# A new order for an attention-and-gMLP block: modulation products between identity products, Silu written as tanh, the last tile in unequal pieces

## The chip, the cores and the metric

One Trainium2 chip, one of its cores. The metric is the device time of one execution in microseconds (us); the time before is the median of three runs. The engines are named as in the profile: PE (TensorE, with PEld for its weight loads), DVE (VectorE), ACT (ScalarE), POOL (GpSimd), SP (SyncE, which here only issues DMAs).

## What is computed

A block with adaptive layer norm: S = 2048 rows, D = 448 columns, 16 heads of 28, a causal window of 256 keys, and a gated MLP of half-width 896 with a full S x S spatial product.

```
mod = silu(c) @ w_mod                      # 1 x 6*448: sa, ca, ga, sb, cb, gb
h = layernorm(x) * (1 + ca) + sa
q, k, v = split(h @ wqkv)                  # 16 heads of 28
p = softmax(mask(q k^T / sqrt(28)))        # key j of query i: 0 <= i - j < 256
x = x + ga * ((p @ v) @ wo)
h = layernorm(x) * (1 + cb) + sb
z = gelu(h @ w_in)                         # 2048 x 1792
z1, z2 = z[:, :896], layernorm(z[:, 896:])
g = w_sp @ z2 + b_sp
x = x + gb * ((z1 * g) @ w_out)
```

## The kernel before

The rows are cut into 16 tiles of 128, four tiles to a tile block. Every step (a product, a copy out of PSUM, a DMA) is recorded as an operation with the engines that may run it. A string, `ORDER` (lines 19 to 74), then lists all operations in sequence, each as a word of number, engine and buffer slots: "623.p.0" is operation 623 on PE with its first choice of bank. Each engine runs its own words in exactly that order, and waits by semaphores for what an operation needs. So the string alone decides on which engine a step runs and what stands in front of it.

The head loads x, the packed QKV weights and w_mod. Products of the identity with itself (L559) run on PE while nothing else is ready. The row c is turned into a column by four small products (L524), ACT applies Silu (L528, L529), and 32 products with the chunks of w_mod (L538) make the modulation column modT (L550, L551). The layer norm of a tile is statistics on DVE (L603, L606), a power on POOL (L611), a shift (L615) that only ACT's form of the norm needs, and the norm itself on DVE (L623), ACT (L625) or POOL (L628). QKV weights are copied into a padded layout WQK (L594, L595).

Tile block 0 goes in halves of two tiles: PE transposes xn (L679), the modulation is applied while hT is written out of PSUM (ACT L686, DVE L688), and QK products of 256 columns (L726) follow with the four chunks of D in the sequence 0, 1, 2, 3; their results go to qT and KT (L753, L754). Block 1 is transposed by PE too (L701, evicted at L715). Blocks 2 and 3 are transposed by DMA from SP's queue (L481, hT<-xn) and then modulated in place (L669 on ACT, L671 on DVE or POOL); their QKV products are L764, with copies out at L774 (ACT) and L775 (DVE). For block 3, K is copied in finer pieces (L793, L794). V is made at L801 and copied at L805 (ACT) and L806 (DVE).

Attention is S products (L876), exps on ACT (L909, L940), masks on DVE (L919, L955, L958), products with V (L984), a division (L997, L999), a DMA transpose of o_sb, the output product (L1007) and the residual (L1012). The second norm and its modulation (L1030 on ACT, L1032 on DVE or POOL) follow the same pattern. Then z2 and its gelu (L1063, L1074, L1086), z1 (L1109, L1117), the spatial products (L1133) against w_sp, which comes through 32 DMA transposes (wspA, wspB, also L481 on SP), the output products (L1152), the last sums (L1163, DVE) and the stores (L1168, SP). The last tile's output is made in three column pieces, 0 to 224, 224 to 336 and 336 to 448.

SP runs its DMA issues in order as well: a transpose of w_sp listed early is issued early.

Of the kernel before, what the change touches and what calls it, by code (L numbers as in the profile page):

```python
# [19 lines left out]
2.a 30.v 40.g 41.g 42.g 0.s 31.v 32.v 33.v 43.g 44.g 3.a 4.s 38.g 34.v 5.s 35.v 36.v 37.v 45.g 6.s 59.p.0 60.p.0 52.p.0 54.a 53.a 7.s 51.a 61.p.1 46.g  # L20
146.v 8.s 62.p.1 63.p.0 147.v 1.s 140.v 64.p.0 148.g 9.s 141.v 149.g 65.p.0 142.v 10.s 66.p.0 143.g 150.v 151.a.0 67.p.0 68.p.0 69.p.0 70.p.0 11.s
39.g 144.v 56.p.0 145.v.1 134.g 14.s 57.p 58.p 12.s 167.p.1 132.a 114.v 164.p.2 113.v 133.v 135.g 73.p.3 168.v 16.s 74.p.0 165.v 75.p.0 169.a 152.v
13.s 176.p.0.3 166.a 177.p.4.5 15.s 153.v 158.v 154.g 178.p 179.p 137.a 155.g 17.s 180.p 159.v 181.p 160.v 136.v 185.p 161.g 156.v 183.p 182.p 189.a
190.p.1.2 187.v 191.p.6.7 138.g 157.a.0 162.v 192.p 193.p 163.v.1 139.g 170.p.3 173.p.5 171.v 194.p 234.v 172.v 230.v 228.v 235.v 55.v 231.v 232.v
229.v 233.v 195.p 184.p 198.p 196.p 197.p 174.a 175.a 199.p 186.a 204.p.3 200.a 208.a 203.a 206.p.0 205.p.5 207.p.3 220.p.1 209.v 188.v 211.v 202.a
201.a 210.a 376.p.0.0 377.a.0 378.a 222.p.0 226.p.6 368.p.0.1 221.v 47.g 48.g 236.g 49.g 50.g 237.g 238.v 240.v.0 239.v.1 241.g.2 223.v 242.v.3 227.v
212.p.0 216.v 246.p.1 243.p.4 247.v 244.v 248.v 369.a.0 370.a 372.p.0.2 373.a 374.a 213.p.0 275.v 217.v 245.v 371.v 273.v 277.v 375.v 274.v 115.p.1
380.p.0.1 381.a.1 116.a 382.a 29.s 840.s 20.s 841.s 18.s 846.s 214.p.0 249.p.3 251.p.4 218.a 250.a 384.p.0.3 215.p.7 253.p.0 255.p.3 385.a 252.a 386.a
388.v 279.v 278.v 379.v 280.v 276.v 219.v 397.p.0.1 263.p.4 271.p.1 281.g 282.g 383.v 256.v 283.v 254.v 326.v 324.v 264.v 272.v 398.a.0 399.a
389.p.0.2 224.p.0 257.p.2 285.g.0 284.g.1 286.g.2 287.g.3 390.a.2 391.a 393.p.0.0 394.a 259.p.1 260.a 395.a 225.v 387.v 258.v 400.v 392.v 261.p.0  # L30
401.p.0.1 262.v 552.p.0 535.p.3 536.p 537.p 538.p 569.p.2 570.p 553.p 554.p 539.v 396.v 402.a.3 403.a 405.p.0.4 571.p 555.p 269.p.2 572.p 540.v.0
409.v 556.v 406.a 270.a 407.a 418.p.0.3 419.a.0 404.v 557.v.1 267.p.2 26.s 118.s 21.s 842.s 117.s 19.s 119.s 289.s 288.s 120.s 291.s 290.s 121.s 124.s
123.s 558.s 586.p.0 265.p.0 408.v 268.v 322.v 266.v 410.p.0.1 587.p 588.p 589.p 295.a 293.g 294.g 292.v 300.p.0 573.v 323.v 574.v.2 590.v 320.v 301.v
411.a.0 420.a 414.p.0.0 412.a 296.p.1 302.p.0 415.a 416.a 129.g 130.g 128.g 131.g 325.v 591.v.1 297.v 327.v 321.v 303.v 421.v 413.v 328.g 329.g 417.v
422.p.0.1 423.a.1 575.s 125.s 541.s 845.s 592.s 298.p.1 306.p.0 426.p.0.0 299.a 424.a 427.a 304.p.1 603.p.0 604.p 605.p 606.p 431.p.0.1 307.a 428.a
542.p.0 310.p.4 432.a.2 433.a 430.v 425.v 330.v 607.v 305.v 608.v.0 543.v 311.v 544.v 331.g.0 332.g.1 333.g.2 334.g.3 439.p.0.2 440.a.0 441.a 620.p.3
308.p.0 621.p 435.p.0.0 436.a 437.a 429.v 545.v 309.v 434.v 622.p 593.p.0 623.p 443.p.0.1 444.a.3 445.a 312.p.3 314.p.4 442.v 624.v 594.v 625.v.1
595.v 438.v 315.v 843.s 336.s 338.s 337.s 609.s 335.s 626.s 447.p.0.3 448.a 313.a 449.a 637.p.4 638.p 559.p.2 639.p 460.p.0.0 461.a.1 462.a 451.v
560.v 446.v 610.p.3 654.p.1 640.p 596.v 450.v 611.v 641.v 341.g 597.g 612.v 642.v.2 561.v 452.p.0.3 655.p 656.p 657.p 576.p.3 339.g 658.v 577.v 562.v
659.v.1 546.g 340.g 342.g 598.g 599.g 453.a.0 454.a 456.p.0.0 318.p.0 627.p.1 457.a 458.a 464.p.0.1 465.a.1 455.v 613.v 563.g 547.g 548.g 628.v 564.g  # L40
565.g 463.v 600.g.0 349.p.3 343.p.1 468.p.0.0 350.a 469.a 466.a 470.a 566.g.1 319.v 578.v 344.v 459.v 671.p.4 672.p 347.p.3 348.v 472.v 481.p.0.3
345.p.2 316.p.4 673.p 674.p 482.a.0 346.a 483.a 473.p.0.1 474.a.2 475.a 351.p.3 467.v 317.v 471.v 688.p.3 689.p 23.s 839.s 25.s 27.s 122.s 643.s 24.s
629.v 675.v 352.v 676.v.0 601.g 614.g 549.g.2 567.g 550.g 660.s 602.s 477.p.0.0 690.p 691.p 355.p.0 478.a 479.a 485.p.0.1 486.a.3 487.a 644.p.3
353.p.4 476.v 579.v 484.v 580.g 581.g 356.v 480.v 645.v 489.p.0.4 490.a 491.a 705.p.0 706.p 707.p 708.p 582.g 583.g.0 615.g 584.g 692.v 630.v 354.v
693.v.1 493.v 494.p.0.0 495.a.0 496.a 363.p.1 661.p.0 502.p.0.1 492.v 709.v 631.g 632.g 616.g 488.v 710.v.2 662.v 633.g 497.v 28.s 551.s 126.s 127.g
844.s 677.s 364.v 722.p.0 723.p 678.p.4 679.v 503.a.0 504.a 498.p.0.4 724.p 725.p 359.p.1 499.a 500.a 506.p.0.0 507.a.1 505.v 726.v 727.v.0 634.g.2
360.v 501.v 663.v 514.v 635.g 585.s 694.s 568.s 22.s 728.s 711.s 357.p.2 361.p.0 358.a 510.p.0.2 511.a 739.p.3 740.p 741.p 742.p 508.a 523.p.0.1
695.p.4 646.v 743.v 744.v.1 729.p.1 362.v 696.v 664.v 647.v 648.v 730.v 524.a.0 512.a 515.p.0.4 365.p.4 712.p.1 516.a.2 815.g 617.g.0 816.g 814.g
649.g 650.g 513.v 509.v 618.v 680.v 713.v 366.a 519.p.0.2 517.a 520.a 525.a 756.p.2 757.p 758.p 759.p 527.p.0.3 521.a 528.a.3 531.a 529.a 532.a 745.s
636.s 619.s 746.p.0 651.g.1 652.g 518.v 817.g 863.p.2 864.p.0 865.p 866.p 681.v 760.v 761.v.0 526.v 530.v 665.g 666.g 667.g 682.g 683.g 534.v 522.v  # L50
668.v.0 533.v 669.g 790.p.2 791.p 773.p.3 792.p 793.p 774.p 775.p 776.p 731.v 747.v 794.v 762.s 367.s 653.s 875.a 867.a 763.p.0 670.s 684.g 685.g.2
686.g 795.v.0 697.v 732.v 698.v 733.v 777.v 699.g 700.g 714.v 813.g 778.v.1 764.v 701.v 715.v 734.g 735.g 702.v.1 748.v 703.v 736.v.0 881.p.1 882.p.0
883.p 884.p 1003.p.2 1004.p.3 1005.p 1006.p 819.a 821.a 820.a 885.a 892.a 737.g 818.g 687.s 796.s 779.s 1008.a 1009.a 1007.a 898.p.1 899.p.0 900.p
901.p 1010.a 910.a 902.a 780.p.0 797.p.1 916.p.0 917.p.1 918.p 919.p 704.s 869.v 765.v 766.v 767.v 876.v 886.v 716.g 717.g 718.g 719.v.2 738.s 720.v
810.g 768.g 887.v 769.v 749.v 750.v 893.v 894.a.0 770.v.1 751.g 752.g 771.v 888.v 753.g.0 781.v 889.v 782.v 721.s 783.v 825.v 822.g 824.a 830.s 772.s
# [211 lines left out]
def bass_adaLN_cond__sliding_block__mixer_gmlp__prompt_kernel(  # L267
# [15 lines left out]
    NT = S // 128  # L283
# [361 lines left out]
    for tb in range(NB4):  # L645
# [84 lines left out]
        for hf in range(2 if tb == 0 else 0):  # L730
            for qk in range(2):
# [4 lines left out]
                if hf == 0:  # L736
# [6 lines left out]
                    for g in four:  # L743
                        last[g] = pe(MMH, [part(g, DC - 1, hq[g], hf)], [evh[hf], t_wqk[qk], done_], vv + 0.03 + 0.001 * g)
# [492 lines left out]
```

## Time and profile before

| what | before |
|---|---|
| median of 3 runs | 272.44 us (271.46 to 273.02) |
| the profiled execution's own time | 273.21 us |
| its span | 271.5 us |
| busy share of the span: PE, DVE, ACT, POOL | 96%, 59%, 49%, 46% |
| granted clock of TensorE | 1.00 |
| first QK product of block 0 | 8.62 us |
| DMA moved | 25.46 MB |

Time and span differ by 1.7 us, which lie outside of the profiled stretch. The busy shares are means over very different stages: the stretches that the prediction shows count for more. "PE busy" includes the identity products at the start, which compute nothing.

### The profile page before, as it was taken

The page shows a single profiled execution, that of the slowest core. Times are in us where ns is not written, and L with a number is a line of the kernel's source. Part 1 is how long each engine was busy: PE and PEld are TensorE (multiplying, and loading weights), DVE is VectorE, ACT ScalarE, POOL GpSimd, SP SyncE. Part 2 cuts the span into 40 slices and gives each one's busy share as a digit, 9 for nine tenths or more (in the row PEclk, how much of TensorE's full clock was granted, in tenths as well). Part 3 has the DMA queues.
Part 4 walks back from the last instruction along what each step waited for, and adds up shares of the span by engine and source line. Part 5 has one row for each costly group of instructions (what it writes and reads, how often), then busy time and mean ns, then how long its engine had stood idle before and what let it go on. Part 6 is the DMA issues. An engine that isn't in the chain of part 4 may idle for free.

```text
span 271.5 us, 6856 instructions
## 1 busy us (share of the span) xinstructions
PE 262.0 (96%) x2918; PEld 135.5 (50%) x2918; DVE 160.2 (59%) x357; ACT 132.2 (49%) x189; POOL 124.9 (46%) x184
## 2 busy tenths in 40 slices
PE   7898999999999999999999999999999999999995
PEld 3654455556476656444444444444444444444453
DVE  6898999999999999885746111123212102251233
ACT  3598999999999994799988300000000000000000
POOL 8530619325949668762499033445313100464130
PEclk9999999999999999999999999999999999999999
DMA  7998532857943567875999970000000000100203
GB/s 224 304 277 171 141 84 46 111 86 117 187 95 80 87 70 161 99 157 106 167 181 195 173 151 0 0 4 0 17 0 2 0 0 0 53 17 0 68 19 101
DMA packets 66777, 25.46 MB, mean 94 GB/s; under 512 B 57845, under 2 KB 66042, under 8 KB 66746
## 3 DMA queue, kind: packets, MB, share of 16 engines
q1 hardware_dynamic: 66472, 24.56, 47.1%
q8 instruction: 23, 0.38, 0.6%
q10 hardware_dynamic: 274, 0.46, 0.5%
q14 instruction: 8, 0.07, 0.1%
HBM read 9.53 MB, written 1.84 MB: 42 GB/s over the span
## 4 chain that ended last, share of the span: by engine, by line
PE 65%; DVE 21%; POOL 5%; ACT 5%; DMA 2%; issue 1%; DVEq 0%; POOLq 0%
PE ps L1133 36%; PE ps L1152 8%; PE ps L1109 7%; PE ps L1063 6%; DVE PA L919 4%; DVE PA L955 3%; DVE st_all L603 3%; PE ps L764 2%; ACT PA L909 2%; POOL rs_all L611 2%; DMA hT<-xn 2%; DVE Vaug L806 2%; PE ps L876 1%; PE ps L1007 1%; DVE o_sb L999 1%
## 5 line engine op out<-in xcount | busy, mean ns | idle before, releaser
L1140 POOL TENSOR_TENSOR z1T<-tmpg,z1T 128x512 bf16<-128x512 bf16 x28 | 31.8, 1154 | 76.2 <-DVE tmpg L1137 76.2
L909 ACT ACTIVATE PA<-ps 128x1536 bf16<-128x1536 f32 (+4 forms) x64 | 60.4, 974 | 2.7 <-PE ps L876 1.7
L1137 DVE TENSOR_TENSOR tmpg<-ps,bsp_bc 128x512 bf16<-128x512 f32 x28 | 19.0, 689 | 62.4 <-PE ps L1133 58.2
L1133 PE MATMUL ps<-wspB,z 128*128 128x512 bf16 x224 | 49.3, 379 | 0.0
L1133 PE MATMUL ps<-wspA,z 128*128 128x512 bf16 x224 | 49.2, 379 | 0.0
L1133 PEld LDWEIGHTS ps<-wspA,z 128*128 128x128 bf16 x224 | 21.8, 98 | 26.5 <-issue 0.4
L1133 PEld LDWEIGHTS ps<-wspB,z 128*128 128x128 bf16 x224 | 21.9, 98 | 26.3
L1163 DVE TENSOR_TENSOR fin<-ps,x_sb 128x448 bf16<-128x448 f32 (+2 forms) x18 | 10.0, 569 | 28.7 <-PE ps L1152 28.7
L611 POOL TENSOR_TENSOR rs_all<-ve_all,neghalf 128x1 f32<-128x1 f32 (+1 forms) x31 | 22.6, 732 | 5.2 <-DVE ve_all L608 3.3
L984 PEld LDWEIGHTS ps<-Vaug,PA 128*128 128x128 bf16 x720 | 20.4, 96 | 5.3 <-issue 1.3
L984 PE MATMUL ps<-Vaug,PA 128*128 128x32 bf16 x720 | 22.2, 176 | 0.4 <-DVE x_sb L1012 0.2
L1063 PE MATMUL ps<-w_in,hT 64*128 64x448 bf16 x224 | 22.3, 349 | 0.2 <-ACT z L1074 0.2
L1152 PE MATMUL ps<-w_out_g,z1T 128*128 128x448 bf16 (+2 forms) x126 | 22.2, 332 | 0.0
L1109 PE MATMUL ps<-hT,w_in 64*128 64x512 bf16 x196 | 21.8, 376 | 0.0
L919 DVE TENSOR_TENSOR PA<-PA,mask 128x1024 bf16<-128x1024 bf16 (+1 forms) x32 | 21.7, 683 | 0.0
L764 PE MATMUL ps<-hT,WQK 128*128 128x512 bf16 x80 | 19.6, 380 | 0.5 <-DVE hT L671 0.5
L603 DVE BATCH_NORM_STATS2 st_all<-x_sb 128x6 f32<-128x448 bf16 x32 | 19.3, 611 | 0.0
L876 PE MATMUL ps<-qT,KT 32*64 32x64 bf16 (+3 forms) x768 | 17.9, 223 | 0.9 <-ACT PA L909 0.3
L608 POOL TENSOR_SCALAR ve_all<-mv_all 128x1 f32<-128x1 f32 (+1 forms) x19 | 6.5, 344 | 25.2 <-DVE mv_all L606 21.0
L940 ACT ACTIVATE PA<-ps 128x1536 bf16<-128x1536 f32 (+1 forms) x16 | 16.4, 1027 | 1.7 <-PE ps L876 1.5
L955 DVE TENSOR_TENSOR PA<-PA,mask 128x2048 bf16<-128x2048 bf16 x14 | 17.0, 1215 | 0.0
L1152 PEld LDWEIGHTS ps<-w_out_g,z1T 128*128 128x128 bf16 x126 | 11.7, 98 | 10.1 <-POOL z1T L1140 0.2
(115 smaller groups left out, 334.7 us busy)
## 6 DMA issues: line engine op xcount, KB each, us to landing
w_in<-in_B_w_in_dram SPq DMA_DIRECT2D x8, 224.0 KB, 4.1
out_dram<-fin SPq DMA_DIRECT2D x15, 112.0 KB, 1.7
x_sb<-in_A_x_dram SPq DMA_DIRECT2D x3, 448.0 KB, 5.3
wmod<-in_w_mod_dram SPq DMA_DIRECT2D x1, 1344.0 KB, 9.7
w_out_g<-in_B_w_out_dram SPq DMA_DIRECT2D x1, 784.0 KB, 5.1
bsp_bc<-in_B_b_sp_dram SPq DMA_DIRECT2D x1, 512.0 KB, 4.3
x_sb<-in_A_x_dram SPq DMA_DIRECT2D x2, 224.0 KB, 3.4
wmod<-in_w_mod_dram SPq DMA_DIRECT2D x2, 224.0 KB, 5.3
```

The costliest lines, as they stand in the source:

```text
L603: st = [dve(0.62 if True else 0, lambda e, t=t, ci=ci, s=s: e.bn_stats(st_all[:, slot, t, ci, :], s()), deps(t), prio) for ci, s in enumer ...
L611: rs = pool(0.41 + 0.155 * len(tiles), lambda e: e.tensor_tensor(rs_all[:, slot, a:b], ve_all[:, slot, a:b], neghalf[:, 0:b - a], ALU.pow) ...
L764: m = pe(4 * MMS, [lambda e, h=h, g=g, kc=kc, tb=tb: e.matmul(ps[:, h.slot[0], :], lhsT=WQK[:, kc, 4 * g:4 * g + 4, :].rearrange("p a b -> ...
L909: return e.activation(cols(place(kb, hf) + 64 + 768 * a, [[384, 2 * (b - a)], [1, w]]), ps[:, h.slot[0]:h.slot[0] + b - a, 2 * n * w:(2 * ...
L919: main_mk[(kb, hf)] = dve(0.15 + 512 * tri / 1920.0, lambda e, hf=hf, tri=tri: e.tensor_tensor(cols(place(kb, hf) + 64, [[384, 8], [192, t ...
L955: return e.tensor_tensor(cols(a, [[d, 2], [384, 16], [1, 64]]), cols(src(), [[0, 2], [64, 16], [1, 64]]), mask_ap([[64 if m else 192, 2], ...
L984: fns.append(lambda e, hO=hO, hd=hd, bi=bi, kb=kb, nb=nb, j=j, c=(2 * t + k) * 384 + 128 * (j - kb), half=half: e.matmul(ps[:, hO.slot[0], ...
L1063: return lambda e, kc, p0, start, stop: e.matmul(ps[:, hs[t % 2].slot[hf], 0:D], lhsT=hT[p0:p0 + 64, kc, t * 128:(t + 1) * 128], rhs=w_in[ ...
L1109: return lambda e, kc, p0, start, stop: e.matmul(ps[:, hs[b // 2].slot[b % 2], :], lhsT=w_in[p0:p0 + 64, kc, ft * 128:(ft + 1) * 128], rhs ...
L1133: m = pe(16 * MMS, [lambda e, h=h, si=si, ft=ft, tb=tb: e.matmul(ps[:, h.slot[0], :], lhsT=z2[:, si, ft * 128:(ft + 1) * 128], rhs=(wspA i ...
L1140: u = pool(1.16, lambda e, ht=ht, ft=ft, tb=tb: e.tensor_tensor(z1T[tb][:, ft, :], tmpg[:, ht.slot[0], :], z1T[tb][:, ft, :], ALU.mult), [ ...
L1152: return [lambda e, ft=ft: e.matmul(ps[:, h.slot[0], c0:c1], lhsT=z1T[t // 4][:, ft, (t % 4) * 128:(t % 4 + 1) * 128], rhs=w_out_g[:, ft, ...
```

## The change

There are six edits, of which the new order holds the most.

1. `c_row` is padded to four full chunks and the constant `one` becomes 0.5, so that PSUM holds c/2. ACT takes its tanh (in the table set that the exps use), and one DVE instruction makes (tanh + 1) times c/2, which is silu(c). One load of a table set falls away.
2. The identity products are cut differently (`warm(9, ...)`, `warm(45, ...)`: 17 in all instead of 15), and the products with w_mod run partly between them, chunk by chunk.
3. In tile block 0 the odd tiles' norm runs only on DVE, and needs no shift. The copies out of the transposes are paired as chunks (2, 0) and (1, 3).
4. The QK products of block 0 take the chunks in the sequence 2, 1, 0, 3.
5. The last tile's pieces are 0 to 224, 224 to 384 and 384 to 448, and the middle piece's store is issued by ACT's queue.
6. `ORDER` is new throughout. A main mask may run on POOL by the new code; the new order doesn't use that.

```diff
-    t_p1 = [dve(0.1, lambda e: e.memset(one[:], 1.0), prio=-99.0), dve(0.1, lambda e: e.memset(sc_sb[:], 0.0), prio=-98.9)]
+    t_p1 = [dve(0.1, lambda e: e.memset(one[:], 0.5), prio=-99.0), dve(0.1, lambda e: e.memset(c_row[:, D:DP], 0.0), prio=-98.9)]
...
-    t_sc = [
-        act(0.25, lambda e: e.activation(sc_sb[:, 0:3], ps[:, hC.slot[0], 0:3], ACT.Silu), [t_cT, t_p1], -90.0, table="silu"),
-        act(0.25, lambda e: e.activation(sc_sb[0:64, 3:4], ps[0:64, hC.slot[0], 3:4], ACT.Silu), [t_cT, t_p1], -90.0, table="silu"),
-    ]
-    hC.until += t_sc
+    t_th = act(0.25, lambda e: e.activation(th[:], ps[:, hC.slot[0], 0:DC], ACT.Tanh), [t_cT], -90.0, table="exp")
+    t_sc = dve(0.2, lambda e: e.scalar_tensor_tensor(sc_sb[:], th[:], 1.0, ps[:, hC.slot[0], 0:DC], ALU.add, ALU.mult), [t_th], -90.0)
+    hC.until += [t_th, t_sc]
...
-    warm(14, [], 0.44, 1)
-    warm(40, [], 0.22, 1)
+    warm(9, [], 0.43, 1)
+    warm(45, [], 0.215, 1)
...
+        if not share and t % 2:
+            return add({"dve": (0.39, on_dve)}, deps, prio, [h])
...
-            for cp in range(2):
+            for cp, chs in enumerate(((2, 0), (1, 3))):
...
+        FIRST = (2, 1, 0, 3)
+
         def part(g, kc, h, hf):
             return lambda e: e.matmul(ps[:, h.slot[0], 0:256], lhsT=WQK[:, kc, 4 * g:4 * g + 4, :].rearrange("p a b -> p (a b)"),
-                                      rhs=hT[:, kc, hf * 256:(hf + 1) * 256], start=(kc == 0), stop=(kc == DC - 1))
+                                      rhs=hT[:, kc, hf * 256:(hf + 1) * 256], start=(kc == FIRST[0]), stop=(kc == FIRST[-1]))
...
-            for c0, c1 in ((0, D // 2), (D // 2, 3 * D // 4), (3 * D // 4, D)) if t == NT - 1 else ((0, D),):
+            for c0, c1 in ((0, D // 2), (D // 2, D - 64), (D - 64, D)) if t == NT - 1 else ((0, D),):
...
-                o = add({"sp": (0.4, lambda e, hf=hf, t=t, c0=c0, c1=c1: e.dma_start(out_d[:, t, c0:c1], fin[:, hf.slot[0], c0:c1]))},
+                o = add({"act" if c0 == D // 2 else "sp": (0.4, lambda e, hf=hf, t=t, c0=c0, c1=c1: e.dma_start(out_d[:, t, c0:c1], fin[:, hf.slot[0], c0:c1]))},
```

Of the order itself, three places. First PE's queue in the head (ident is the identity, L559 or L558 its products with itself; wmod the modulation weights; L679 or L680 the transposes of block 0; WQK the QK weights). Before:

```order
L559 MATMUL ps<-ident 128x512 x10
L542 MATMUL ps<-xn,ident 128x8
L538 MATMUL ps<-sc_sb,wmod 128x1 x32
L679 MATMUL ps<-ident,xn 128x128 x8
L559 MATMUL ps<-ident 128x512 x3
L726 MATMUL ps<-hT,WQK 128x256 x23
L679 MATMUL ps<-ident,xn 128x128 x8
L726 MATMUL ps<-hT,WQK 128x256 x25
```

and now:

```order
L558 MATMUL ps<-ident 128x512 x6
L541 MATMUL ps<-xn,ident 128x8
L537 MATMUL ps<-sc_sb,wmod 128x1 x8
L558 MATMUL ps<-ident 128x512 x3
L537 MATMUL ps<-sc_sb,wmod 128x1 x24
L680 MATMUL ps<-ident,xn 128x128 x8
L558 MATMUL ps<-ident 128x512 x2
L729 MATMUL ps<-hT,WQK 128x256 x12
L558 MATMUL ps<-ident 128x512
L729 MATMUL ps<-hT,WQK 128x256 x2
```

Eight products with w_mod moved ahead of three identity products, and some identity products moved in among the first QK products.

Second, SP's queue behind the head's first loads (wspA is half of w_sp, wo_g the output weights of the attention, mod_rows a copy of the gates in DRAM). Before:

```order
L409 DMA x_sb<-in_A_x_dram 128x4x448
L450 DMA wo_g<-in_A_wo_dram 64x448
L481 DMA_TRANSPOSE wspA<-in_B_w_sp_dram 128x1024
L405 DMA wo_g<-in_A_wo_dram 64x448
L481 DMA_TRANSPOSE wspA<-in_B_w_sp_dram 128x1024
L409 DMA x_sb<-in_A_x_dram 128x4x448
L481 DMA_TRANSPOSE wspA<-in_B_w_sp_dram 128x1024
L445 DMA w_in<-in_B_w_in_dram 128x896
```

and now:

```order
L410 DMA x_sb<-in_A_x_dram 128x4x448
L406 DMA wo_g<-in_A_wo_dram 64x448
L410 DMA x_sb<-in_A_x_dram 128x4x448
L405 DMA wo_g<-in_A_wo_dram 128x3x448
L576 DMA mod_rows<-gg_sb 1x448 x4
L451 DMA wo_g<-in_A_wo_dram 64x448
L576 DMA gg_sb<-mod_rows 128x448
L576 DMA modT<-mod_rows 128x3x1
L482 DMA_TRANSPOSE hT<-xn 128x4x128 x4
```

The transposes of w_sp moved behind the loads of x, the gates and the first transposes of hT.

Third, POOL's queue once block 2's norms begin (L628 or L629 the norm, L671 or L672 the modulation of hT, L587 or L586 the gate on the output weights). Before:

```order
L628 TENSOR_SCALAR xn<-x_sb,rs_all,ve_all 128x448
L608 TENSOR_SCALAR ve_all<-mv_all 128x4
L611 TENSOR_TENSOR rs_all<-ve_all,neghalf 128x4
L628 TENSOR_SCALAR xn<-x_sb,rs_all,ve_all 128x448 x4
L671 TENSOR_SCALAR hT<-hT,modT 128x512 x2
L587 TENSOR_TENSOR wo_g<-wo_g,gg_sb 128x448 x4
L608 TENSOR_SCALAR ve_all<-mv_all 128x4
L611 TENSOR_TENSOR rs_all<-ve_all,neghalf 128x4
L628 TENSOR_SCALAR xn<-x_sb,rs_all,ve_all 128x448 x4
```

and now:

```order
L607 TENSOR_SCALAR ve_all<-mv_all 128x4
L610 TENSOR_TENSOR rs_all<-ve_all,neghalf 128x4
L629 TENSOR_SCALAR xn<-x_sb,rs_all,ve_all 128x448 x2
L586 TENSOR_TENSOR wo_g<-wo_g,gg_sb 128x448 x4
L607 TENSOR_SCALAR ve_all<-mv_all 128x4
L610 TENSOR_TENSOR rs_all<-ve_all,neghalf 128x4
L629 TENSOR_SCALAR xn<-x_sb,rs_all,ve_all 128x448 x2
L672 TENSOR_SCALAR hT<-hT,modT 128x512 x2
```

The other two norms of each block and most of the modulation moved to DVE's queue. Over the attention, up to the last mask, DVE has 11 steps of the norm on tiles of x instead of 5 and 6 modulations of hT instead of 1, and gives copies out of PSUM to ACT: KT in 512 columns 4 instead of 6, KT in finer pieces 2 instead of 4, qT in 512 columns 6 instead of 7, V 10 instead of 12.

More of the change, by code (lines that the diff above doesn't have):

```diff
@@ L24 @@
[L24 to L31, printed above, removed]
@@ L518, in bass_adaLN_cond__sliding_block__mixer_gmlp__prompt_kernel @@
     t_mask.append(pool(0.2, lambda e: e.tensor_copy(mask01[:, 4, :], mask01[:, 0, :]), [t_mask[0]], -84.0))
-    t_pre = act(0.2, lambda e: e.activation(zero[:, 1:2], zero[:, 0:1], ACT.Silu), [t_p0], -98.8, table="silu")
+    t_pre = act(0.2, lambda e: e.activation(zero[:, 1:2], zero[:, 0:1], ACT.Tanh), [t_p0], -98.8, table="exp")
     hC = Hold(bM)
-    t_cT = pe(0.5, [lambda e, ch=ch, m=m: e.matmul(
-        ps[0:m, hC.slot[0], ch:ch + 1], lhsT=c_row[:, ch * 128:ch * 128 + m], rhs=one[:, 0:1], start=True, stop=True)
-        for ch, m in ((0, 128), (1, 128), (2, 128), (3, 64))], [t_c, t_p1[0]], -91.0, [hC])
-    t_sc = [
-        act(0.25, lambda e: e.activation(sc_sb[:, 0:3], ps[:, hC.slot[0], 0:3], ACT.Silu), [t_cT, t_p1], -90.0, table="silu"),
-        act(0.25, lambda e: e.activation(sc_sb[0:64, 3:4], ps[0:64, hC.slot[0], 3:4], ACT.Silu), [t_cT, t_p1], -90.0, table="silu"),
-    ]
-    hC.until += t_sc
+    t_cT = pe(0.5, [lambda e, ch=ch: e.matmul(
+        ps[:, hC.slot[0], ch:ch + 1], lhsT=c_row[:, ch * 128:ch * 128 + 128], rhs=one[:, 0:1], start=True, stop=True)
+        for ch in range(DC)], [t_c, t_p1], -91.0, [hC])
+    t_th = act(0.25, lambda e: e.activation(th[:], ps[:, hC.slot[0], 0:DC], ACT.Tanh), [t_cT], -90.0, table="exp")
+    t_sc = dve(0.2, lambda e: e.scalar_tensor_tensor(sc_sb[:], th[:], 1.0, ps[:, hC.slot[0], 0:DC], ALU.add, ALU.mult), [t_th], -90.0)
+    hC.until += [t_th, t_sc]
     t_screp = dve(0.5, lambda e: e.tensor_copy(sc_rep[:], sc_sb[:].unsqueeze(2).broadcast_to([128, DC, 32])), [t_sc, t_x[1]], -16.0)
@@ L652, in bass_adaLN_cond__sliding_block__mixer_gmlp__prompt_kernel @@
             tiles = [4 * tb + i for i in half]
-            r = stats(0, tiles, lambda t: [lambda: x_sb[:, t, :]], lambda t: [t_x[t // 4] if t >= 4 else t_x0[t // 2]], v_e)
+            r = stats(0, tiles, lambda t: [lambda: x_sb[:, t, :]], lambda t: [t_x[t // 4] if t >= 4 else t_x0[t // 2]], v_e, tb > 0 or tiles[0] % 2 == 0)
             for t in tiles:
```

126 lines of the change are left out of this document (68 added, 58 removed).

## The prediction

> **What bounds the kernel now.** I read the page's first part, then the busy time by stretches, then the chain that ended last, then the waits of the stretches in which TensorE is not full. The stretches (columns: stretch, length, busy time and count of PE, PEld, DVE, ACT, POOL, granted clock, DMA share, GB/s):
> ```profile
> 8.60:25.00 16.40, 13.63 (x197) 8.82 (x197) 14.04 (x39) 12.63 (x21) 5.50 (x12) 1.00 1.15 273
> 25.00:100.00 75.00, 73.25 (x1502) 42.86 (x1499) 74.30 (x144) 71.99 (x83) 42.32 (x58) 1.00 0.58 99
> 114.50:150.50 36.00, 36.00 (x345) 16.81 (x346) 24.19 (x75) 32.51 (x61) 22.85 (x44) 1.00 0.94 161
> 150.50:268.40 117.90, 117.90 (x576) 55.43 (x574) 27.64 (x44) 2.56 (x5) 35.74 (x32) 1.00 0.13 30
> 268.40:271.50 3.10, 0.18 (x4) 0.01 (x1) 0.62 (x3) 0.00 (x0) 0.00 (x0) 1.00 0.26 74
> ```
> From 114.5 to 268.4 TensorE has no gap, 153.9 us in two rows, and the granted clock is 1.00 throughout. The change leaves the work of that stretch as it is, so nothing can be won there. What can move is the head (16.40 − 13.63 = 2.8 us without TensorE work), the attention (25 to 100), where PE, DVE and ACT are all full to within 3.0 us, and the 3.1 us of the tail. POOL is the one engine with room in the attention: 42.32 of 75. The chain through the head and the tail (start, length, what):
> ```profile
> 7.32 0.41 PE ps L679 x4
> 9.36 1.28 PE ps L726 x10
> 11.09 0.35 DVE ve_all L615
> 11.46 0.90 DVE xn L623
> 12.40 0.41 PE ps L679 x4
> 21.38 1.09 issue
> 268.27 0.37 DVE fin L1163 x2
> ```
> The second half of the transposes of tile block 0 waits for one DVE norm of 0.90 us (L623, tile 3), and at 21.38 TensorE's queue stands 1.09 us for nothing that the profile shows. TensorE's own timeline gives the waits beside them:
> ```profile
> 12.40 0.62 PE L679 MATMUL ps<-ident,xn 128*128 128x128 bf16 x8 [0.80 <-DVE xn L623]
> 12.86 1.15 PE L726 MATMUL ps<-hT,WQK 128*128 128x256 bf16 x9
> 14.28 1.92 PE L726 MATMUL ps<-hT,WQK 128*128 128x256 bf16 x16 [0.27 <-ACT hT L686]
> 22.47 0.23 PE L701 MATMUL ps<-ident,xn 128*128 128x128 bf16 x1 [1.09 <-issue]
> ```
>
> **The change part by part.** All terms are against the profiled execution, 273.21 us, which lies 0.77 above the median of 272.44; the sum is then put onto the median.
>
> *Head, modulation products and Silu.* The products as such and the ACT work are the same size; Silu as tanh loads one table set fewer. That load was off the path:
> ```profile
> 16.43 1.28 ACT L940 ACT_TABLE_LOAD   x1
> 18.09 2.08 ACT L940 ACTIVATE PA<-ps 128x1536 bf16<-128x1536 f32 x2 [0.38 <-PE ps L876]
> 7.32 0.62 PE L679 MATMUL ps<-ident,xn 128*128 128x128 bf16 x8
> 7.78 0.81 PE L559 MATMUL ps<-ident 128*128 128x512 bf16 x3
> ```
> The first exp waited after the load for TensorE (0.38), so the 1.28 us are worth nothing at that place; they free ACT for evictions, which I count in the attention. The three identity products at 7.78 fill the time until hT is there; in the new order nine products of this kind stand ahead of the first transposes after the c products, and six more behind these transposes and among the first QK products. Each costs 0.27 by that row, and they stand where TensorE would wait for hT: 0, and up to +0.5 if two of them delay a ready product. Starting QK with chunk 2 moves which eviction is first, not how many: 0 (±0.2).
>
> *Head, norms.* Tile 3's norm waits for a shift step (L615) that only ACT's form of the norm needs; without it DVE saves part of the 0.35 row. But DVE now makes three of the first hT evictions instead of two ahead of the statistics of tiles 2 and 3, which puts those about 0.35 later, and ACT no longer takes a norm. POOL has one WQK copy less beside the norm of 0.90. Against this stands the row of that form over the whole run:
> ```profile
> L623 DVE TENSOR_SCALAR xn<-x_sb,mv_all,rs_all 128x448 bf16<-128x448 bf16 x12 | 6.3, 535 | 0.7 <-DMA hT<-xn 0.4 <-POOL ve_all L618 0.2
> L671 DVE TENSOR_SCALAR hT<-hT,modT 128x512 bf16<-128x512 bf16 x1 | 1.2, 1202 | 0.0
> L1032 DVE TENSOR_SCALAR hT<-hT,modT 128x512 bf16<-128x512 bf16 x5 | 1.8, 402 | 0.0
> ```
> A norm of the mean 0.535 instead of 0.90 gives −0.37. I take −0.3 for the second transposes, between 0 and −0.7. The wait ahead of 14.28 (the gap between the end of the row at 12.86 and it is 0.27) goes if the evictions pair as (2,0) and (1,3) with one of each pair on DVE: −0.3 (0 to −0.4).
>
> *The queue that stands at 21.38.* The transfers in that window (queue, packets, MB, share; the issue and its time to landing):
> ```profile
> q1 hardware_dynamic: 3712, 1.68, 122.7%
> q8 instruction: 1, 0.02, 0.8%
> wspA<-in_B_w_sp_dram SPq DMA_TRANSPOSE x3, 6.2
> ```
> Three transposes of the spatial weights are in the DMA engines from 16 to 24 us, and the one block of code of that window comes through the same engines. The new order issues none of them until the transposes of hT for tile block 2 are out, so I read the gap as code that came late, and take it as gone: −1.1 (0 to −1.1). The Trainium skill, Runtime: NRT & Kernel Launch, section Instruction fetch mechanics, says that a sequencer fetches its next page on a queue of its own while it executes, and that this is hidden by the pace of issue. By that sentence the gap would be something else and would stay, and the sum below would be 1.1 us less; the row at 21.38 speaks against full hiding, but does not name its cause. What the moved transposes cost: they now land during the attention (DMA share 0.58), and behind the last transposes of hT the new order leaves 19 of this kind where 23 stood, ahead of the spatial products that read them; I take 0, and up to +1 if the last ones come late.
>
> *Attention.* These are the steps that change engine (line, engine, form, count, total and mean ns):
> ```profile
> L774 ACT ACTIVATE qT<-ps 128x512 bf16<-128x512 f32 x5 | 3.1, 621 | 0.0
> L774 ACT ACTIVATE KT<-ps 128x512 bf16<-128x512 f32 x2 | 1.2, 610 | 0.0
> L805 ACT ACTIVATE Vaug<-ps 128x448 bf16<-128x448 f32 x4 | 2.2, 545 | 0.0
> L775 DVE CAST KT<-ps 128x512 bf16<-128x512 f32 x6 | 4.1, 676 | 0.1
> L806 DVE CAST Vaug<-ps 128x448 bf16<-128x448 f32 x12 | 7.2, 611 | 0.0
> L671 POOL TENSOR_SCALAR hT<-hT,modT 128x512 bf16<-128x512 bf16 x6 | 6.3, 1052 | 12.8 <-DMA hT<-xn 12.8
> L628 POOL TENSOR_SCALAR xn<-x_sb,rs_all,ve_all 128x448 bf16<-128x448 bf16 x18 | 13.9, 782 | 4.4 <-DVE ve_all L615 4.0
> ```
> DVE takes over 11 tensor_scalar steps up to the attention's last mask (xn from 5 to 11, hT from 1 to 6): 11 x 0.402 = 4.4 us at the free price, 11 x 0.535 = 5.9 at the norm's mean. It gives off four KT casts, of which two are of the finer form, and one of qT, 5 x 0.676 = 3.4, and two of Vaug, 2 x 0.611 = 1.2: net 0 to +1.3. ACT takes what DVE gave off, 5 x 0.61 + 2 x 0.545 = 4.1 by the means (records of one engine overlap at their ends, so 3.3 is the least), against 75 − 71.99 = 3.0 us of its idle time in the stretch. If all of the idle time could be used the end comes 0.3 to 1.1 later; if none, 3 to 4; and as the first exps come earlier (no table load ahead of them, other products first), some of it starts before 25. I take +0.9, between −1 and +3. POOL's relief, some 11 x 0.8 to 1.0 us, is worth nothing by itself.
>
> *Transition and tail.*
> ```profile
> ACT z L1086 <- PE ps L984: 3.4, 1, 3.4
> 267.91 1.94 SPq L1168 DMA_DIRECT2D out_dram<-fin  x4
> 267.82 0.75 PE L1152 MATMUL ps<-w_out_g,z1T 128*128 128x112 bf16 x12
> 268.27 0.75 DVE L1163 TENSOR_TENSOR fin<-ps,x_sb 128x112 bf16<-128x112 f32 x3 [0.39 <-PE ps L1152]
> ```
> ACT waits 3.4 us ahead of the first gelu; the new order has it modulate hT in that hole: −0.2 (0 to −0.4). At the end SP issues four stores back to back, 1.94/4 = 0.48 each, and the last of three pieces stands behind two others. With the middle piece on ACT's queue the last one issues one slot earlier, −0.48, and its DVE piece is 64 columns instead of 112; against that, the middle piece is larger (160 columns). I take −0.4 (−0.6 to +0.1).
>
> The sum: −0.3 − 0.3 − 1.1 + 0.9 − 0.2 − 0.4 = −1.4. From 273.21 that is 271.8, and put on the median, 272.44 − 1.4 = **271.0** us. Adding the helpful and the harmful ends by squares rather than singly gives about −3 to +1 for this case, 269.4 to 273.4.
>
> **The rivals.** *DVE's moved steps are blocked by POOL.* DVE's one L671 step ran beside two POOL products:
> ```profile
> 43.00 2.04 POOL L587 TENSOR_TENSOR wo_g<-wo_g,gg_sb 128x448 bf16<-128x448 bf16 x2
> 43.99 1.20 DVE L671 TENSOR_SCALAR hT<-hT,modT 128x512 bf16<-128x512 bf16 x1
> ```
> It took 1.202 us where the same shape at L1032 takes 0.402: a loss of 0.80 a step. The change puts 11 more such steps on DVE inside the stretch in which DVE has 0.7 us of room (74.30 of 75). If every second one loses, 5.5 x 0.80 = 4.4, less the 1.4: +3.0, **275.4**. It decides from 4 of 11 on (3.2 − 1.4 = +1.8, over 0.5%). For it: those rows. Against: the mean of 0.535 over twelve norms is a loss of 0.13 each, by which 11 lose 1.5, and POOL has less to do afterwards. The Trainium skill, SBUF — State Buffer, section Who interferes with whom, says that a tensor_scalar of the fast kind and GpSimd take one pair of ports as an exclusive lock, so that whoever issues second waits out the whole instruction; the 1.202 us agrees with it, being about the free time plus a POOL step, and it speaks against this change. Chance 0.30.
>
> *Only the tail moves.* The head's gain is taken back because DVE and ACT set the attention's end in any case; what stays is −0.4: **272.0**. For it: both engines are full from 25 to 100. Against: their work starts earlier with the head. Chance 0.12.
>
> *POOL's relief counts in full.* If POOL's serial work (xn, then hT) was what delayed the QKV products of blocks 2 and 3, the 3.0 us of idle time of ACT and the 1.75 us of PE in the stretch go, and the head's 2.8 too: about −4, **268.4**. For it: a POOL step is 0.782 and 1.052 where DVE needs 0.40. Against: DVE has little room to take it. Chance 0.18.
>
> **How the numbers follow.** A measurement of this kernel can tell about 0.5%, 1.36 us, from no change: 271.08 and 273.80 are the bounds. The forecast has 0.40; its centre lies at the lower bound, so 0.24 of that is faster, 0.14 within, 0.02 slower. Faster: 0.24 + 0.18 from the third rival = 0.42. Within: 0.14 + 0.12 from the tail rival + 0.02 from the mild end of the first = 0.28. Slower: 0.02 + 0.28 = 0.30. The likeliest case alone spans 269.4 to 273.4; the range of 8 in 10 reaches down to the third rival's centre and up just past the first's, 268.4 to 275.6.
>
> **What would show it.** Right: second L680 group near 12.0 and no issue gap of 1 us near 21; DVE's xn and hT tensor_scalar rows at 0.40 to 0.55; the gap-free stretch of TensorE beginning about a microsecond earlier; the last store issued by 0.7 us after TensorE's end. The first rival: those DVE rows at 0.8 to 1.2 and masks late, and the exps ending later than before. The tail rival: the exps end where they did. Wrong altogether: a gap in TensorE between 114 and 268, which no term here has, for instance from spatial weights that land late, or a head in which QK starts later than 8.6.

## The result: slower by 1.0%

| | before | after |
|---|---|---|
| median | 272.48 us (270.91 to 273.02, 6 runs) | 274.88 us (273.28 to 276.65, 6 runs) |
| ratio, 95% interval | | 1.0103 (1.0054 to 1.0151) |
| profiled execution, span | 273.21, 271.5 | 273.28, 271.4 |

The changed kernel is about 2.8 us slower, with an interval of 1.5 to 4.1. Its profiled execution happens to be the fastest of its six, and that of before was slower than each of its six: the two traces end at the same moment, and alone they would show no change. So a second trace was taken of the changed kernel (below, 276.06). Executions more than 1.5% slower than the fastest of the same kernel are left out of the ratios and their intervals, while the medians and ranges hold all executions.

The busy time by stretches in the first trace after (columns as in the prediction):

```profile
8.60:25.00 16.40, 15.96 (x273) 10.58 (x274) 15.54 (x46) 13.63 (x26) 5.45 (x12) 1.00 0.76 234
25.00:100.00 75.00, 69.60 (x1449) 41.83 (x1456) 73.03 (x149) 72.35 (x84) 33.29 (x46) 1.00 0.59 105
100.00:114.50 14.50, 14.50 (x218) 8.33 (x220) 13.59 (x34) 10.80 (x19) 9.03 (x15) 1.00 1.01 172
114.50:150.50 36.00, 35.57 (x340) 16.47 (x338) 24.94 (x72) 31.38 (x60) 24.59 (x50) 1.00 0.95 163
150.50:268.40 117.90, 117.27 (x557) 54.80 (x564) 27.71 (x43) 2.47 (x5) 33.66 (x30) 1.00 0.13 26
```

The head has become dense (15.96 of 16.40 where before had 13.63), though identity products are in it. What it won is gone by 100: TensorE has 69.60 of 75 where it had 73.25 (some missing records may be in that difference). DVE and ACT are nearly as full as before (73.03 against 74.30, 72.35 against 71.99), and POOL has 9 us less to do. From 114.5 on TensorE's rows are 1.1 us short of full, with 24 records fewer than before.

DVE's moved steps, grouped by form (count, total us, mean ns), in the same trace:

```profile
L622 DVE TENSOR_SCALAR xn<-x_sb,mv_all,rs_all 128x448 bf16<-128x448 bf16 x21 | 8.8, 432 | 1.9 <-POOL ve_all L617 1.0 <-POOL rs_all L610 0.6
L672 DVE TENSOR_SCALAR hT<-hT,modT 128x512 bf16<-128x512 bf16 x4 | 2.1, 543 | 0.0
L1036 DVE TENSOR_SCALAR hT<-hT,modT 128x512 bf16<-128x512 bf16 x8 | 2.8, 384 | 0.0
```

They are at 0.38 to 0.54, near the free price, not at 0.8 to 1.2: the broad form of the first rival did not happen here. DVE now waits 1.9 us ahead of norms, though (0.7 before), most of it for small steps on POOL.

The tail, in the timeline:

```profile
267.73 1.65 DVE L1167 TENSOR_TENSOR fin<-ps,x_sb 128x448 bf16<-128x448 f32 x4 [0.70 <-PE ps L1156]
269.24 0.37 ACTq L1172 DMA_DIRECT2D out_dram<-fin  x1
```

TensorE ends at 269.05 and the span at 271.44, 2.39 us later; before it was 268.58 and 271.46, 2.88. The tail gained 0.49.

### The profile page after: what moved, and what is told of

Its sections match the earlier page's. It is cut to its first block, busy times and chain, and to the rows that moved or that the text cites. A ratio compares the mean times of both kernels' runs of the same rounds, so it can differ in the third digit from the quotient of the medians.

```text
span 271.4 us, 6838 instructions
## 1 busy us (share of the span) xinstructions
PE 260.4 (96%) x2901; PEld 135.9 (50%) x2920; DVE 161.3 (59%) x365; ACT 134.5 (50%) x195; POOL 111.0 (41%) x167
## 4 chain that ended last, share of the span: by engine, by line
PE 70%; DVE 18%; ACT 6%; POOL 4%; issue 2%; POOLq 0%; DVEq 0%
PE ps L1137 35%; PE ps L1156 8%; PE ps L1067 8%; PE ps L1113 6%; ACT PA L912 4%; DVE PA L922 3%; PE ps L1011 3%; PE ps L988 2%; DVE st_all L602 2%; DVE PA L959 2%; POOL rs_all L610 2%; PE ps L558 2%; DVE xn L622 2%; DVE Vaug L809 1%; PE ps L879 1%
## 5 line engine op out<-in xcount | busy, mean ns | idle before, releaser
L1156 PE MATMUL ps<-w_out_g,z1T 128*128 128x448 bf16 (+3 forms) x126 | 22.0, 332 | 0.0
L988 PE MATMUL ps<-Vaug,PA 128*128 128x32 bf16 x720 | 21.6, 176 | 0.4 <-DVE PA L959 0.3
L607 POOL TENSOR_SCALAR ve_all<-mv_all 128x1 f32<-128x1 f32 (+1 forms) x20 | 5.3, 267 | 34.8 <-DVE mv_all L605 34.1
L767 PE MATMUL ps<-hT,WQK 128*128 128x512 bf16 x71 | 18.0, 380 | 1.4 <-DVE hT L672 0.6
L1167 DVE TENSOR_TENSOR fin<-ps,x_sb 128x448 bf16<-128x448 f32 (+3 forms) x18 | 10.0, 570 | 11.3 <-PE ps L1156 9.2
```

What stands on the lines that cost most here:

```text
L988: fns.append(lambda e, hO=hO, hd=hd, bi=bi, kb=kb, nb=nb, j=j, c=(2 * t + k) * 384 + 128 * (j - kb), half=half: e.matmul(ps[:, hO.slot[0], ...
L1156: return [lambda e, ft=ft: e.matmul(ps[:, h.slot[0], c0:c1], lhsT=z1T[t // 4][:, ft, (t % 4) * 128:(t % 4 + 1) * 128], rhs=w_out_g[:, ft, ...
```

## The experiments

Theory A: DVE (with ACT) sets the end of the attention, whatever the head does, and the new order gives them more. Theory B: POOL holds DVE's steps. Theory C: moved transfers hold up those that TensorE waits for. All times are medians, with ratios against the kernel before of the same call.

**A second trace of the changed kernel.** No edit.

> The changed kernel once more, for a second trace. Theory A (DVE and ACT set the attention's end, and the new order loads both more): the trace looks like the first one, exps end near 103.2, span 271 to 274, time 273.3 to 276.7. Theory B (DVE and POOL block each other by chance): a longer execution shows DVE's tensor_scalar steps (xn, hT) at 0.6 us or more on average, where the first trace has 0.43. Theory C (the moved transposes of w_sp hold up the transposes that attention needs): a longer execution shows waits for hT<-xn or hT<-o_sb that the first trace does not have.

275.69 us, ratio 1.0104 (1.0065 to 1.0142). TensorE at the second transposes of block 0, in the first trace and in the second:

```profile
11.88 0.62 PE L680 MATMUL ps<-ident,xn 128*128 128x128 bf16 x8 [0.26 <-DVE xn L622]
...
13.63 0.62 PE L680 MATMUL ps<-ident,xn 128*128 128x128 bf16 x8 [1.56 <-DVE xn L622]
```

DVE's two norms ahead of them in the first trace, then in the second, with what POOL did there in the second:

```profile
10.88 0.95 DVE L622 TENSOR_SCALAR xn<-x_sb,mv_all,rs_all 128x448 bf16<-128x448 bf16 x2
...
11.32 2.25 DVE L622 TENSOR_SCALAR xn<-x_sb,mv_all,rs_all 128x448 bf16<-128x448 bf16 x2
11.59 0.56 POOL L594 COPY WQK<-wq_st 128x448 bf16<-128x448 bf16 x1
12.08 1.21 POOL L509 MEMSET Vaug<- 128x256 bf16 x1
```

The same two norms take 0.95 or 2.25; the second of them takes 0.49 or 1.78. In the slow case it starts while POOL's copy runs and ends at 13.57, after the memset's end at 13.29. The old order had that memset at 3.5 us (L508 in the chain of before); the new one has it right behind the copy. The first exp begins at 15.86 in one trace and at 17.60 in the other; 0.44 of this is there at the first transposes already (7.22 and 7.66). Theory B in the form that was expected, 0.6 us on average, did not come true: the norms' mean is 0.49. It holds for one step in the head, and that falls one way or the other from run to run. Theory C's sign was there too: in the second trace TensorE waits 0.71 us for hT<-o_sb at 110, in the first it does not.

**The tail alone.** In the kernel before:

```diff
-... ((0, D // 2), (D // 2, 3 * D // 4), (3 * D // 4, D)) ...     1197.v.2 1193.v.3 1198.s 1194.s 1201.v.1 1202.s
+... ((0, D // 2), (D // 2, D - 64), (D - 64, D)) ...             1193.v.3 1194.s 1197.v.2 1198.a 1201.v.1 1202.s
```

> The kernel before with edit 5 alone (pieces 224, 160, 64, the middle store on ACT's queue). Prediction's term: -0.4 us, 272.0 to 272.1 where before has 272.4. A rival in which the tail makes up the loss: +0.5 or more.

271.34 us, 0.9968 (0.9943 to 0.9993): −0.9 us. The trace has 2.39 us from TensorE's end to the span's, as in the changed kernel, so the tail accounts for 0.5 of it there; the rest lies within the interval (0.2 to 1.6 us).

**Silu as tanh alone.** In the kernel before, edit 1, with `54.a 53.a` in the order now `53.a 54.v`.

> The kernel before with edit 1 alone (Silu as tanh, one table load fewer). Prediction's term: 0, ACT's exps may begin up to 0.4 us earlier; -0.5 to +0.2 us. If the table load mattered: -1 us.

272.04 us, 0.9986 (0.9967 to 1.0005): not told from no change. These two kernels keep the old order, with its early transposes of w_sp, and give two more looks at the place where TensorE's queue stood 1.09 us (the tail's kernel first):

```profile
20.42 1.18 PE L701 MATMUL ps<-ident,xn 128*128 128x128 bf16 x16
...
20.89 1.06 PE L700 MATMUL ps<-ident,xn 128*128 128x128 bf16 x16
```

All 16 products run as one row, without the gap. Two more traces with the old order, further down, don't have it either: it was seen in one execution of the five that were profiled, and the order does not force it.

**The new head before the old rest.** The changed code, the first 190 words of the new order, then the old order for what is left.

> The changed code with the first 190 words of the new order (the head, to the first exps) and then the old order for all that is left, the new tail at the end. Theory A: keeps the head's gain of 2 us in the first exp and loses nothing in the attention: 269.5 to 271, exps end near 101. A rival in which the head's gain can't be kept whatever follows (attention bounded by data or by a queue): 272 to 273, exps end at 103.

273.12 us, 1.003 (1.0002 to 1.0057), above what either theory expected. Its norms take 2.25 us too, and the first exp begins at 17.36: little of the head's gain is left. Inconclusive on theory A until the memset is out of the way.

**The memset back at its place.** In the changed kernel:

```diff
-... 4.s 38.g 34.v ...   172.v 46.g 191.p ...
+... 4.s 38.g 46.g 34.v ...   172.v 191.p ...
```

> The changed kernel with one POOL memset (Vaug, L509, 1.2 to 1.36 us) moved from behind tile 3's WQK copy to its place in the old order, ahead of the first powers. Theory B in the head (DVE's second norm of block 0's second half is held by that memset: 1.78 us in the second trace, 0.49 in the first): the norm takes under 1.0, the second transposes start by 12.9 instead of 13.6, first exp by 16.8 or earlier, and 0.7 to 1.3 us of that reach the end: 274.0 to 274.6 where the changed kernel has 275.2. Theory A (DVE and ACT set the attention's end whatever the head does): 275.2, unchanged.

273.94 us, 1.0068 (1.0041 to 1.0094), 0.36% below the changed kernel's 1.0104, or 1.0 us; the two intervals overlap. The two norms:

```profile
10.73 1.15 DVE L622 TENSOR_SCALAR xn<-x_sb,mv_all,rs_all 128x448 bf16<-128x448 bf16 x2
```

The first exp begins at 15.90. That the memset held the norm is shown by these traces (1.78 us behind it, 0.68 without it). What it cost in time is about 1 us by the ratios, the size that was expected, but not clear of their intervals.

**The engines back, the places kept.** In the changed kernel, 61 words of the attention get the engine of the old order, for instance

```diff
-252.a ... 291.v ... 329.v.1 ... 615.v.0
+252.v ... 291.g ... 329.g.1 ... 615.g.0
```

> The changed kernel, its order kept, but the 61 steps from the first normalised tiles of block 1 to the second norm's modulation that had changed engine put back on their old engine (evictions from ACT to DVE, norms and modulations from DVE to POOL). Theory A: ACT's work between first and last exp falls from 84.2 to about 80.7 and DVE's from 85.2 to about 82.5, the stretch from 87.5 to about 84, time 271.5 to 272.7. Rival (the places in the order cost the time, not the engines): the stretch stays at 87 or grows, 274.5 to 278.

282.75 us, 1.0376 (1.0333 to 1.0419), 7.5 us worse. **Only the norms and modulations back:**

> The same with only the 44 steps of norm and modulation put back (mostly from DVE to POOL), the evictions left on ACT as in the new order. Theory A: DVE's work falls to about 79 to 80, ACT's stays at 84.2, so ACT alone bounds the stretch, 86 to 87: 273.8 to 275. Rival that DVE alone matters (its steps held by POOL): stretch 83 to 84, 271.5 to 272.5.

280.69 us, 1.0327 (1.0279 to 1.0376). **The reverse, the new engines in the old order:**

> The kernel before, its order kept, with those 61 steps on the engines that the new order gives them. Theory A: ACT 84, DVE 85 of work between first and last exp, +2.5 to +3.5: 275 to 276. Rival (the places matter, not the engines): 272.0 to 273. If POOL's relief were worth its price: 270 to 271.5.

293.87 us, 1.0793 (1.0743 to 1.0844). All three are far slower than any forecast for them, the rivals' too (engines back at most 278, norms back 275, the reverse 276): an engine and a place in the order belong together, so neither can be put back alone. The stretches from the span's start to the end of the last exp, engines back and then the reverse:

```profile
0.00:112.92 112.92, 98.43 (x1855) 58.23 (x1865) 98.93 (x208) 90.78 (x115) 58.84 (x94) 0.98 0.61 130
0.00:118.14 118.14, 97.52 (x1817) 57.06 (x1826) 97.62 (x221) 95.39 (x122) 39.07 (x74) 0.99 0.59 119
```

DVE's work is 98.9 and 97.6 us, as ever, but DVE stands idle 14.0 and 20.5 us. TensorE's longest wait in the first of them is of the kind one would expect: it waits once for a modulation that POOL does where the order reckoned with DVE.

```profile
PE ps L767 <- POOL hT L672: 3.7, 1, 3.7
PEld ps L767 <- POOL hT L672: 3.5, 1, 3.5
```

These runs therefore say nothing on the price of the moved work itself.

**More work on DVE, more work on ACT.** Both in the kernel with the memset moved:

```diff
+    for i, n in enumerate(...):   # six copies of the attention on DVE; in the other kernel eight on ACT
+        ways["dve"] = (cost, [lambda e, i=3 * i + k: e.bn_stats(junk[:, i, :], ident[:]) for k in range(3)] + [f])
+        ways["act"] = (cost, [lambda e, i=i: e.activation(junk[:, i, :]..., ident[:]..., ACT.Copy), f])
```

> after_vaug_early with 18 small DVE instructions added in the attention (statistics of the identity into unused memory, three ahead of each of six copies; 18 x about 0.19 = 3.4 us; result unchanged). Theory A in its form 'DVE is the engine that sets the attention's end': the last exp and the end come about 3 us later, 276.5 to 277.5. Rival 'ACT sets it': under 1.5 us, 274 to 275.4.

276.55 us (+2.6), ratio 1.0143 (1.0093 to 1.0192).

> after_vaug_early with 8 ACT copies of 256 columns added in the attention (of the identity into unused memory, about 0.4 us each, 3.2 us; result unchanged). Theory A in the form 'DVE sets the end': under 1.5 us, 274 to 275.4. Rival 'ACT sets it': about 3 us, 276.5 to 277.2. If both add about 3 us, both are on the path, by turns.

274.74 us (+0.8), 1.008 (1.0051 to 1.0109). And the same DVE instructions **in the old order** (with the new tail and tanh):

> before_tanh_tail (271.6) with the same 18 small DVE instructions added in the attention (3.3 us more of DVE's busy time in dve_more). Theory A (DVE sets the attention's end in the old order too): +2.5 to +3.3, 274.1 to 274.9. Rival (the old order has room on DVE): under +1.5, below 273.1.

273.37 us, +1.75 over its own base of 271.62. Span's start to the end of the last exp, in this sequence: memset moved; with more DVE; with more ACT; old order with tanh and tail; that with more DVE (the third and fourth busy times are DVE and ACT):

```profile
0.00:103.22 103.22, 95.80 (x1855) 57.88 (x1866) 97.66 (x223) 92.66 (x122) 44.54 (x73) 1.00 0.68 138
0.00:106.48 106.48, 96.79 (x1855) 57.99 (x1866) 100.99 (x241) 93.12 (x122) 43.49 (x73) 1.00 0.65 139
0.00:104.35 104.35, 95.89 (x1855) 57.82 (x1866) 98.07 (x224) 94.43 (x130) 43.61 (x73) 1.00 0.69 143
0.00:101.86 101.86, 95.87 (x1819) 56.85 (x1828) 97.16 (x209) 89.42 (x113) 58.15 (x92) 1.00 0.70 139
0.00:103.87 103.87, 96.59 (x1819) 56.62 (x1828) 99.44 (x227) 89.90 (x113) 57.92 (x92) 1.00 0.65 136
```

DVE's 18 instructions add 3.3 us of busy time and put the last exp 3.3 us later in the new order; in the old one they add 2.3 and put it 2.0 later, less than theory A's 2.5 to 3.3 and more than the rival's 1.5. ACT's eight add 1.8 and put it 1.1 later. In each of these rows DVE is idle for only 4 to 6 us out of 102 to 106, and most of that lies in the head (length less DVE's busy time, from the same view cut at 30 us):

| DVE idle, us | before 30 us | from 30 to the end of the last exp |
|---|---|---|
| old order with tanh and tail | 4.33 | 0.36 |
| that with more DVE | 4.20 | 0.23 |
| new order, memset moved | 4.04 | 1.52 |
| that with more DVE | 4.67 | 0.81 |

So DVE is the engine without room from 30 us on, added work on it moves the attention's end nearly in full in both orders, and ACT has a part in it. The added instructions stand ahead of copies that products wait for; a part of the shift may come from that place and not from a full queue.

**Four norms from DVE to POOL.** In the kernel with the memset moved, `615`, `649`, `683` and `751` go from `v` to `g`.

> after_vaug_early with four of the second norm's steps (tiles 4, 6, 8, 12; their users come after the attention) on POOL instead of DVE. Theory A: DVE does 4 x 0.43 = 1.7 us less, and the end comes 1 to 1.7 us earlier: 272.2 to 273. Rival (the order was made for DVE's speed there, POOL's 0.8 comes in the way of its other steps): 274 or more.

274.01 us, 1.0047 (1.0014 to 1.008): inconclusive, the medians are equal and the ratio is 0.2% lower, within the intervals. Theory A had expected 272.2 to 273. In the trace only two of the four norms lay ahead of the last exp, and DVE's busy time up to there fell by 0.2 only (97.46 against 97.66), as the masks took 1.0 us more in all. So DVE was hardly relieved, and the run does not test theory A.

**The head's gain under the old order, memset moved.**

> head_after_rest_before (273.1) with the same POOL memset moved ahead. Theory B: the first exp comes near 15.9 instead of 17.4. Theory A on top of it (DVE has nothing idle that a shorter head could remove): the last exp stays at 101.5 to 103 and the time at 271.6 or more, no better than before_tanh_tail. Rival (the head's 2 us can be kept under the old order): 269.6 to 270.5.

272.27 us, 1.0016 (1.0001 to 1.003). The first exp begins at 16.12, 1.9 us ahead of the old order's 18.03, and the last exp ends at 103.81, 1.9 us behind its 101.86. The time is no better than with tanh and tail on the old order (271.62), as theory A expected, but the last exp comes after the 101.5 to 103 that it gave. The place where the gain goes is not DVE's work (96.88 us against 97.16) but the seam of the two orders. TensorE there, in the run of this kind with the memset still in its way and then in the old order with the new tail:

```profile
26.73 1.67 PE L767 MATMUL ps<-hT,WQK 128*128 128x512 bf16 x7 [1.93 <-DVE hT L716]
...
24.58 1.67 PE L764 MATMUL ps<-hT,WQK 128*128 128x512 bf16 x7
```

With the memset moved the wait is 1.93 us too: DVE stands idle 1.37 us for a product of V, and the last modulation of block 1 stands behind that copy. Block 1's products begin at 25.50, 1.0 us later than with tanh and tail (24.47), and the granted clock is 0.50 from 26 to 28 us in that execution, where the row of seven takes 3.19 us (with the memset still in its way the same wait stands, and the clock is 1.00 from 20 to 30). Like the exchanged engines, these two runs show a place in the order and don't tell what a shorter head is worth.

**Which transfers go first.** With the memset moved, `365.s` (the load of w_out) and `836.s` (a transpose of w_sp) go behind `760.s`, the second of two transposes of o_sb.

> after_vaug_early with two words of SP's queue moved: the load of w_out (784 KB) and one transpose of w_sp now stand behind the transposes of o_sb for tiles 12 and 13 instead of ahead of them. Theory C (those transposes take 5 to 6 us beside the load where they took 2.4 in the old order, and TensorE waits 1.1 to 1.6 us for them near 110 us): they take 2.4 to 4 us, that wait falls under 0.5, the way from the last exp to the end from 169 to 168, time 272.7 to 273.3 where after_vaug_early had 273.9. Rival (the wait is made up before the spatial products, or another transfer takes its place): 273.9.

275.01 us, 1.0109 (1.0072 to 1.0146). TensorE's waits behind the attention, memset moved and then this kernel:

```profile
109.54 0.93 PE L1011 MATMUL ps<-wo_g,hT 128*128 128x448 bf16 x4 [1.55 <-DMA hT<-o_sb]
...
114.77 4.15 PE L1067 MATMUL ps<-w_in,hT 64*128 64x448 bf16 x42 [1.61 <-DVE x_sb L1016]
```

and the transposes of o_sb between 98 and 112 us in the same two and in the old order with tanh and tail (count, us from issue to landing):

```profile
hT<-o_sb SPq DMA_TRANSPOSE x4, 4.7
...
hT<-o_sb SPq DMA_TRANSPOSE x2, 3.0
...
hT<-o_sb SPq DMA_TRANSPOSE x3, 3.3
```

In six traces with the new order's sequence the transposes of o_sb take 4.2 to 5.6 us, in five with the old one 2.5 to 3.3. Here they became as quick as in the old order, so what stands ahead of them in the queue is shown to slow them. The wait is absent too, but four of the six traces don't have one over 0.5 us either, and a wait of the same size stands 5 us later. The run was not faster: the worth is not shown.

**Tanh and tail on the old order.**

> The kernel before with edits 1 and 5 only (tanh, tail), order and engines as before. If the two single results add (-0.9 for the tail, -0.4 for tanh): 270.8 to 271.2, and faster than both kernels. If the tail's store and the shorter head share one gain: 271.4.

271.62 us, 0.996 (0.9933 to 0.9986): faster than both kernels, by 0.4% and 1.4%. The tail alone gave as much; whether the two parts add can't be told, as the single ratios make 0.9954 and the interval is 0.9933 to 0.9986.

## Why the prediction was wrong

It said 271.0 with a chance of 0.42 for faster; the time rose by 2.8 us. Its range held the time, because of the first rival. Three of its signs of being right were there in the first trace (second transposes at 11.88, no gap near 21, DVE's rows at 0.38 to 0.54), and the kernel was slower all the same: none of them was a sign of the attention's end. Two steps of the sum failed: a gap of one execution was taken for one of the order, and the head's gain was carried through the attention in full.

- *The queue that stands at 21.38 (−1.1).* This term was the main one, and there was nothing to win: the gap was in one of the five traces with the old order. The working had said that the profiled execution lay 0.77 above the median, and did not ask which of its gaps made it so. What caused the gap stays open: the block of code of that window began to move at 19.9 us in that trace, 1.4 us ahead of the gap, and between 16.0 and 18.7 in the other four, so it was late there, but no run shows that TensorE waited for it.
- *Head, norms (−0.3).* The sign was wrong in two traces of three: with the memset there, the second transposes begin at 13.4 and 13.6 us, and at 11.88 in the third, where the five traces with the old order have 12.3 to 12.9. I had read which norms moved and which WQK copy left POOL's queue, and not the memset that came in its stead. The first rival had the mechanism right and the place and size wrong: one step, held for 1.3 us, not 11 steps losing 0.80 each. The Trainium skill, SBUF — State Buffer, section Who interferes with whom, has such a step wait out a whole GpSimd instruction. The second trace agrees, and shows two in a row: the norm waited behind the copy and then behind the memset.
- *Head, pairing of the evictions (−0.3).* Right in size: the 0.27 us ahead of 14.28 are gone, the QK products behind the second transposes run as one row of 3.13 us in every trace of the new head.
- *Attention (+0.9).* The sum credited the head's gain in full and charged +0.9 for the copies on ACT, as if an earlier first exp brought an earlier last one. With the memset out of the way the first exp is 2.1 us earlier and the last one 1.4 us later than with tanh and tail on the old order (15.90 and 103.22 against 18.03 and 101.86). The engine without room is DVE, and the new head took only 0.3 us off its idle time before 30 us (4.33 to 4.04). Of the 1.4 us, 0.5 is DVE's busy time (97.66 against 97.16) and 0.9 its idle time: 1.2 more from 30 us on. DVE waits there about 1.0 us for TensorE's products and 0.2 for POOL; which change of place made these waits stays open. The working also undercounted: up to the last exp the traces have 16 norms on DVE instead of 5, not 11, and 6 modulations instead of 1, so 16 steps moved, paid for by fewer casts. The second rival said that the head's gain would be taken back because both engines are full; it was given 0.12, and it was right in that, but not in its 272.0, for the last exp moved back too.
- *The moved transposes of w_sp (0, up to +1).* The place was the right one to doubt, though for a neighbour: the new order has the load of w_out and transposes of w_sp ahead of the last transposes of o_sb, which land in 4.2 to 5.6 us instead of 2.5 to 3.3. TensorE waits 1.1 to 1.6 us there in two of six traces with that order, and no row of the other four shows a wait of 0.5 there. Since taking that wait away brought another, how much of the loss it is stays open.
- *ACT's hole before the first gelu (−0.2).* ACT now modulates hT there, and its idle time ahead of the gelu is 0.66 us instead of 3.36; TensorE was nearly full there before (14.26 of 14.50 from 100 to 114.5), so no worth of it can be read.
- *Tail (−0.4).* Right: 0.49 in the trace, 0.9 by the times with an interval from 0.2 to 1.6.
- *Silu as tanh (0).* Right within what the run can tell.
- *Third rival.* POOL's relief was worth nothing: POOL's busy time up to the last exp fell from 58 to 45 us and the end came later.

In sum: moving the memset gives about 1.0 us of the loss back; the hold is shown, the size is not clear of noise. The remaining kernel is 1.1%, 2.9 us, behind the old order with tanh and tail. In the two traces 1.4 of this is the later end of the attention, and 1.5 the way from there to the end: 169.2 us against 167.6. That way is 167.6 to 167.8 us in three traces of the old order with the new tail and 167.5 to 169.2 in six of the new one, longest where TensorE waits for the transposes of o_sb, so this part differs between executions. The new tail gives 0.5 back.

## What to carry to other kernels

Find the engine whose own busy time fills the stretch, by adding a little work to each and seeing which one moves the end, before crediting a gain ahead of it or a relief beside it. A gain ahead of the stretch counts only as far as it takes idle time off that engine. Take a gap from a single trace as a term only if a second execution has it too, above all when the profiled one was slow. When an order changes, read every instruction that the second engine of a shared pair now has near a critical step, memsets included.

## What the runs showed of the hardware

A POOL memset of 256 columns per partition (1.21 us) held a DVE tensor_scalar that had been waiting behind an earlier POOL copy: the norm took 1.78 us in the second trace and 0.49 in the first, from the same program. With the memset moved away it took 0.68, beside the copy alone. One such neighbour can thus make the same step differ by 1.3 us between executions of one program, and the profiled execution can be either.
